# Retention and a mixture of experts in one kernel: gating products one tile later, weight splits and first expert loads reordered

## The chip, the cores and the metric

The kernel runs on one core of a Trainium2 chip. The metric is the device time of one execution in microseconds (us); the median of several runs is compared.

## The reference

The input is q, k and v for 8 batches, 8 heads, 576 positions and a head size of 64. A causal attention with a decay per head (retention, no softmax) gives 4608 rows of 512 numbers. Each row then goes to one of 8 experts.

```python
scores = scale * np.matmul(q, k.transpose(0, 1, 3, 2))
ret = scores * Dmat[None]                # gamma_h ** (i - j) for i >= j, else 0
x = np.matmul(ret, v)                    # -> rows [4608, 512]
...
logits = x @ w_gate
e_idx = np.argmax(logits, axis=1)
gate_w = softmax(logits)[row, e_idx]     # in the reference: exp, sum + 1e-9
eom = 1.0 / (1.0 + np.exp(-(x @ w_output_gate)))
for e in range(E):
    h = np.maximum(x[mask] @ w1[e], 0.0)           # 512 -> 1024
    ye = h @ w2[e]                                 # 1024 -> 512
    out[mask] = gate_w[mask, None] * eom[mask, e, None] * ye
```

## The kernel before, in words

**Attention.** The rows are worked on in 36 tiles of 128 (`NTILE`). The state of a batch is carried in `st_ps` and copied to `stT`; a cycle of 9 tiles (`CPB`) holds two batches. The order on TensorE, ScalarE, VectorE and SyncE is the order of the program (`tc.manual_schedule()`): each engine takes its instructions in that order and waits where a semaphore is missing. Iteration g does, among other things:

- `scores(g + 1)`: 16 products of 64 x 128 into the two PSUM tiles `sc0` and `sc1` (one buffer each), which VectorE masks into `S_sb`;
- `k_rows(g + 1)`: four transpositions into `k_ps`, copied by ScalarE (not for tiles with g % 9 = 8);
- `xnat(g - 1)`: the transposed output `xT` of the tile before is turned back to rows and multiplied with the gate weights in the same products (into `xa` and `xb`, one buffer each); ScalarE copies the rows to `xgrp`, VectorE the logits to `lg`;
- `outT(g)`: the tile's output into `o_ps`, with the state's part and the masked scores' part; VectorE scales it into `xT`;
- `update(g)`: the state (not in tile g % 9 = 8; tile g % 9 = 0 uses no state).

**Gating** is done for groups of four tiles (`GT`). At the end of iteration 4k, `gate1` finds each row's expert on VectorE and builds `oh` (one-hot rows) and the running counts `c1` and `cum`. `gate2`, two small products on TensorE, counts the rows before each row; it stands in `xnat`, that is in iteration 4k+1, and writes into the free end of `xb`. `gate3`, at the end of the same iteration, makes the slots on VectorE and puts four row scatters into the list `todo`; each later iteration issues one on GpSimd (from iteration 30 on, two). The scatters write the rows, with token number and weight, to the DRAM tensor `xs`, one region per expert. With group 5 (`SNAP`) the kernel fixes expert 0's first 360 slots (`CA`): if fewer rows have come by then, filler rows (`fill`, `zx`) take the rest. So expert 0's first part can be computed before all rows are known.

**Weights.** Expert 0's weights are loaded during the attention and each is split in two parts, `hi` on ScalarE (`hi_w`) and `lo` on VectorE (`lo_w`), in the iterations that `wsched` names: (load, `hi`, `lo`).

**Experts.** All products run as three products of split operands. `transp` makes the transposed, split rows; `mm1(e, part, fb)` makes one of 8 blocks of 128 hidden units for part 0 (360 rows for expert 0, 384 loaded) or part 1 (256 rows) and splits it into `hh` (ScalarE) and `hl` (VectorE); `mm2(e, t)` makes the output of one of five row tiles, which ScalarE scales into `y` and GpSimd scatters to the output. Expert 0's first three row tiles are loaded as whole rows (`load_rows`, `x_g`) and transposed on TensorE; every other row tile is loaded in strided quarters by four DMAs (`load_x`, `x_q`) and transposed on VectorE (L221). The DMAs of `read` wait for every scatter issued so far in the program (`scat`). `fill_slots(e)` issues five filler scatters of expert e on GpSimd.

The functions that the change touches:

Of the kernel before, what the change touches and what calls it, by code (L numbers as in the profile page):

```python
# [23 lines left out]
DM = H * D  # L24
# [23 lines left out]
def tile_retention_moe(  # L48
# [101 lines left out]
    XG, XT, HT = {}, {}, {}  # L150
    scat, todo, at = [], [], {}
    pools = {"xt0": xta, "ht0": hpa}

    def read(**kw):
        i = SP.dma_start(**kw)
# [4 lines left out]
    def load_rows(e, t):  # L160
        XG[e, t] = xg.tile([P, DM], F32, name="x_g")
        o, m = e * NT + ROW0[t], ROWS[t]
        read(out=XG[e, t][0:m], in_=xs[o:o + m, 0:DM])

    def load_x(e, t):
# [7 lines left out]
    def load_idx(e, part):  # L173
        ts = range(TA) if part == 0 else range(TA, CT)
        if e == 0 and part == 0:
            for t in ts:
                o, m = ROW0[t], ROWS[t]
                read(out=idx[0:m, e, t], in_=xs[o:o + m, DM:DM + 2].bitcast(I32))
# [28 lines left out]
    def transp(e, t):  # L207
# [7 lines left out]
        if e == 0 and part == 0:  # L215
            src = pools["ps_h"].tile([P, KB, P], F32, name="h_ps")[:, :, 0:m]
# [9 lines left out]
    def mm1(e, part, fb):  # L226
# [8 lines left out]
        for k in range(KB):  # L235
            for a, b in ((wh, xh), (wh, xl), (wl, xh)):
                T.matmul(ps, lhsT=a[:, k, :], rhs=b[:, k, 0:n], start=(j == 0), stop=(j == 3 * KB - 1))  # L237
# [4 lines left out]
    def mm2(e, t):  # L242
# [6 lines left out]
        for fb in range(FB):  # L249
            wh, wl = (a[:, fb % 2, :] for a in W2[e, fb // 2])  # L250
            hh, hl = HT[e, part, fb]
            for a, b in ((hh, wh), (hh, wl), (hl, wh)):
                T.matmul(ps, lhsT=a[:, n], rhs=b, start=(j == 0), stop=(j == 3 * FB - 1))  # L253
# [55 lines left out]
    def scores(g):  # L309
# [4 lines left out]
        for p in range(NP):  # L314
            for r in range(2):
                q, k = (pk[g][64 * r:64 * r + 64, i, P * p:P * p + P] for i in range(2))
                T.matmul(sc[r][:, p], lhsT=k, rhs=q, start=True, stop=True)  # L317
        for r in range(2):
# [41 lines left out]
    def gate1(n):  # L360
# [14 lines left out]
        zo = sm.tile([P, GT, E], F32, name="zo")  # L375
        V.tensor_tensor(out=zo, in0=z, in1=oh, op=ALU.mult)
        zs = sm.tile([P, GT, 1], F32, name="zs")
        V.tensor_reduce(out=zs, in_=zo, op=ALU.add, axis=AX.X)
# [5 lines left out]
        for t in range(GT):  # L384
            V.tensor_tensor(out=c1[:, t + 1] if t < GT - 1 else cum, in0=c1[:, t], in1=oh[:, t], op=ALU.add)
        ex = sm.tile([P, GT, E], F32, name="ex")
# [14 lines left out]
    def gate3():  # L401
        n, oh, c1, ex, zs = gt.pop("pend")
# [3 lines left out]
        V.tensor_tensor(out=sl, in0=r_ps, in1=bs.broadcast_to([P, GT, E]), op=ALU.add)  # L406
        V.tensor_tensor(out=sl, in0=sl, in1=oh, op=ALU.mult)
# [14 lines left out]
        if n == SNAP:  # L422

            V.tensor_copy(cnt[:, 0], c_ps[:, 0:1])
            todo.extend(fill(0, 1, cnt[:, 0:1], float(CA), TA)[0])
            V.tensor_scalar(out=bump, in0=c_ps[:, 0:1], scalar1=-1.0, scalar2=float(CA), op0=ALU.mult, op1=ALU.add)
# [4 lines left out]
    def xnat(g):  # L431
# [7 lines left out]
        if "pend" in gt:  # L439
            gate2(xb[:, 288:512], False)  # L440
# [14 lines left out]
    for n in (512, 512, 256):  # L455
# [3 lines left out]
    wsched = {(1, 0): (5, 8, 9), (1, 1): (10, 14, 15), (1, 2): (15, 18, 19), (1, 3): (20, 24, 25),  # L459
              (2, 0): (29, 32, 33), (2, 1): (30, 33, 34), (2, 2): (31, 34, 35), (2, 3): (34, 36, 36)}  # L460
# [11 lines left out]
    gap = const.tile([1, 1], F32, name="gap")  # L472
    every = {mybir.EngineType.PE, mybir.EngineType.Activation, mybir.EngineType.DVE, mybir.EngineType.SP}
    with tc.manual_schedule():
        S_next = scores(0)
        k_rows(0)
        for g in range(NTILE):
# [6 lines left out]
            if g == 32:  # L484
                for t in range(TA):
                    load_rows(0, t)
                load_idx(0, 0)
# [78 lines left out]
    mm1(0, 0, 0)  # L566
    gate2(ps_t.tile([P, 512], F32, name="t_ps"), True)
    gate3()
# [161 lines left out]
```

## Time and profile before

| | us |
|---|---|
| median of 3 runs | 649.43 (648.3 to 650.15) |
| the profiled execution | 650.73 |
| its span, first to last instruction | 648.9 |
| TensorE matmuls busy | 621.5 (96%) |
| TensorE weight loads busy | 551.9 (85%) |
| VectorE busy | 358.7 (55%) |
| ScalarE busy | 170.8 (26%) |
| GpSimd busy | 166.9 (26%) |
| mean granted TensorE clock | 0.982 of full speed |

The time of an execution is a little longer than the span. The five engines run side by side, so that busy times don't add up. Matmul records overlap (the next starts while the last still drains), and their ends are modelled. In the rows of the profile PE is TensorE, PEld its weight loads, DVE VectorE, ACT ScalarE, POOL GpSimd and SP SyncE, which issues most DMAs; PEq, SPq and so on are the sequencers. A row of the timeline has the start, the duration, the engine, the line, the operation, what it writes and reads, the shapes, and in brackets the idle time before it with what ended it.

### The profile page before, as it was taken

To read this page: it belongs to the slowest core of one execution; us is meant where nothing else is said; L and a number is where in the kernel's file an instruction comes from. 1 tells how busy PE (TensorE), PEld (TensorE's weight loads), DVE (VectorE), ACT (ScalarE), POOL (GpSimd) and SP (SyncE) were. 2 spreads that over 40 slices of the span, in tenths; PEclk is the share of its full clock that TensorE was granted. 3 is DMA by queue.
4 is the path that set the end of the run, shared out by engine and by line. 5 is a ranking of instruction groups with operands and counts; after the bars stand their busy time and mean duration, and the time that the engine had idled before them with its cause. 6 is when DMAs were issued, how large, how long until landed. Compare 5 with 4: busy or idle time off the path is not lost. (4 is left out here: it accounts for less than half of the span.)

```text
span 648.9 us, 12779 instructions
## 1 busy us (share of the span) xinstructions
PE 621.5 (96%) x5127; PEld 551.9 (85%) x5127; DVE 358.7 (55%) x750; ACT 170.8 (26%) x379; POOL 166.9 (26%) x229
## 2 busy tenths in 40 slices
PE   8999999989969699999999999999999999999995
PEld 6888888878859488997997898799799889979974
DVE  3567787677753237773575286267438518625420
ACT  2333433323431122222222222222222222222210
POOL 2244433545426441401501320150110110010011
PEclk9999999989989699999999999999999999999999
DMA  9867686656424545633364183254417416311001
GB/s 323 275 232 251 219 292 231 215 197 240 147 90 129 141 138 162 188 106 127 115 178 130 59 235 88 82 151 117 143 62 212 126 36 186 123 46 65 0 34 43
DMA packets 55610, 96.24 MB, mean 148 GB/s; under 512 B 14736, under 2 KB 36625, under 8 KB 55548
## 3 DMA queue, kind: packets, MB, share of 16 engines
q1 hardware_dynamic: 45836, 72.99, 37.1%
q0 software_dynamic: 9280, 21.36, 9.0%
q10 hardware_dynamic: 432, 1.05, 0.4%
q8 instruction: 41, 0.67, 0.4%
q14 instruction: 21, 0.17, 0.1%
HBM read 74.02 MB, written 30.64 MB: 161 GB/s over the span
## 5 line engine op out<-in xcount | busy, mean ns | idle before, releaser
L237 PE MATMUL h_ps<-xh,w1h 128*128 128x360 f32 (+1 forms) x512 | 157.1, 307 | 2.9 <-ACT xh L223 2.5
L237 PE MATMUL h_ps<-xl,w1h 128*128 128x360 f32 (+1 forms) x512 | 157.0, 307 | 0.3 <-DVE xl L224 0.3
L237 PE MATMUL h_ps<-xh,w1l 128*128 128x360 f32 (+1 forms) x512 | 156.9, 306 | 0.0
L253 PE MATMUL y_ps<-w2h,hh 128*128 128x512 f32 (+1 forms) x320 | 127.2, 397 | 4.8 <-ACT hh L239 4.8
L257 POOL DMA_INDIRECT out_dram<-y,idx x40 | 39.7, 994 | 346.8 <-ACT y L256 333.8
L253 PE MATMUL y_ps<-w2h,hl 128*128 128x512 f32 (+1 forms) x320 | 126.4, 395 | 1.5 <-issue 1.5
L253 PE MATMUL y_ps<-w2l,hh 128*128 128x512 f32 (+1 forms) x320 | 126.4, 395 | 0.0
L240 DVE SCALAR_TENSOR_TENSOR hl<-h_ps,hh 128x360 fp32r<-128x360 f32 (+1 forms) x128 | 58.7, 475 | 101.1 <-ACT hh L239 99.3
L237 PEld LDWEIGHTS h_ps<-xh,w1h 128*128 128x128 f32 x512 | 97.7, 191 | 3.6 <-ACT xh L223 2.7
L239 ACT ACTIVATE hh<-h_ps 128x360 fp32r<-128x360 f32 (+1 forms) x128 | 54.9, 429 | 171.0 <-PE h_ps L237 151.1
L237 PEld LDWEIGHTS h_ps<-xl,w1h 128*128 128x128 f32 x512 | 97.7, 191 | 1.0 <-DVE xl L224 0.7
L237 PEld LDWEIGHTS h_ps<-xh,w1l 128*128 128x128 f32 x512 | 97.5, 190 | 0.0
L253 PEld LDWEIGHTS y_ps<-w2h,hh 128*128 128x128 f32 (+1 forms) x320 | 59.5, 186 | 20.6 <-ACT hh L239 6.2
L224 DVE TENSOR_TENSOR xl<-x_t,xh 128x512 fp32r<-128x512 f32 x37 | 25.6, 692 | 91.1 <-ACT xh L223 90.4
L253 PEld LDWEIGHTS y_ps<-w2h,hl 128*128 128x128 f32 (+1 forms) x320 | 59.5, 186 | 16.5 <-issue 1.3
L253 PEld LDWEIGHTS y_ps<-w2l,hh 128*128 128x128 f32 (+1 forms) x320 | 59.5, 186 | 14.4
L256 ACT ACTIVATE y<-y_ps,idx 128x512 f32<-128x512 f32 (+1 forms) x40 | 27.6, 690 | 146.7 <-issue 77.2
L319 DVE TENSOR_TENSOR S_sb<-sc,cmat_sb 128x512 f32<-128x512 f32 x72 | 46.1, 682 | 17.9 <-PE sc L317 17.9
L185 POOL DMA_INDIRECT xs<-xgrp,sli x36 | 38.3, 1063 | 66.8 <-ACT xgrp L443 20.9
L306 POOL TENSOR_TENSOR vp<-pk,gk_sb 128x512 f32<-128x512 f32 x36 | 37.6, 1044 | 54.0 <-PE st_ps L333 40.5
L185 POOL DMA_INDIRECT xs<-zx,fill x40 | 47.2, 1180 | 9.5 <-issue 9.4
L317 PE MATMUL sc<-pk 64*128 64x128 f32 x576 | 43.7, 289 | 1.8 <-DVE S_sb L319 1.5
(116 smaller groups left out, 669.9 us busy)
## 6 DMA issues: line engine op xcount, KB each, us to landing
st<-in_w_dram SPq DMA_DIRECT2D x64, 512.0 KB
pk<-in_pack_dram SPq DMA_DIRECT2D x32, 768.0 KB
x_q<-xs SPq DMA_DIRECT2D x148, 64.0 KB
gq_sb<-in_gq_dram SPq DMA_DIRECT2D x5, 256.0 KB
pk<-in_pack_dram SPq DMA_DIRECT2D x4, 256.0 KB
pk<-in_pack_dram SPq DMA_DIRECT2D x2, 512.0 KB
xs<-zx,fill POOLq DMA_INDIRECT x40
out_dram<-y,idx POOLq DMA_INDIRECT x40
```

The source lines that it names most:

```text
L185: i = G.indirect_dma_start(out=xs, out_offset=bass.IndirectOffsetOnAxis(ap=at, axis=0), in_=x, in_offset=None, **({} if bound is None else ...
L224: V.tensor_tensor(out=lo, in0=src, in1=hi.bitcast(F32), op=ALU.subtract)
L237: T.matmul(ps, lhsT=a[:, k, :], rhs=b[:, k, 0:n], start=(j == 0), stop=(j == 3 * KB - 1))
L239: A.activation(out=hh, in_=ps, func=AF.Relu)
L240: V.scalar_tensor_tensor(out=hl, in0=ps, scalar=0.0, in1=hh.bitcast(F32), op0=ALU.max, op1=ALU.subtract)
L253: T.matmul(ps, lhsT=a[:, n], rhs=b, start=(j == 0), stop=(j == 3 * FB - 1))
L256: A.activation(out=y, in_=ps, func=AF.Copy, scale=idx.bitcast(F32)[0:m, e, t, 1:2])
L257: G.indirect_dma_start(out=out, out_offset=bass.IndirectOffsetOnAxis(ap=idx[0:m, e, t, 0:1], axis=0), in_=y, in_offset=None, bounds_check= ...
L306: G.tensor_tensor(out=vs[g], in0=pk[g][:, 2].rearrange("p (h d) -> p h d", h=H), in1=gk_sb[:, g % CPB].broadcast_to([P, H, D]), op=ALU.mult)
L317: T.matmul(sc[r][:, p], lhsT=k, rhs=q, start=True, stop=True)
L319: V.tensor_tensor(out=S_sb[:, r], in0=sc[r], in1=m, op=ALU.mult)
```

## The change

- `gate2` leaves `xnat`. It now stands in `scores`, for the tile with g % 4 = 3, behind the score products, so in iteration 4k+2. `gate3` is cut in two: `gate3a` (the slot sum, and for group 5 the copy of the count) follows it directly, ahead of `S_sb`; `gate3b`, the rest, follows `S_sb`. In `gate1` two operations (`zo`, `zs`) move behind the running counts. The scatters of `todo` are issued behind the next tile's preparation, one per iteration, from iteration 26 on two.
- `wsched` has other iterations for most loads and splits of expert 0's weights.
- Expert 0's first rows are loaded one iteration earlier (31) and wait for the scatters issued by iteration 30 only. Their transpositions, with PSUM space from `k_ps`, move into iterations 34 and 35, ahead of the last tile's `xnat`, and `mm1(0, 0, 0)` and `mm1(0, 0, 1)` are placed around that `xnat` and the last gating.
- Expert 0's row tiles 3 and 4 are now loaded as whole rows too and transposed on TensorE, between its second products.
- Expert 1's x tiles are loaded one by one later; the first of the four DMAs of each waits for a matmul on TensorE (`paced`, `pe[0]`: the first product of the block or second product issued last). Their transpositions move behind expert 0's part 1. Expert 1's first weights are split on ScalarE and VectorE (`hi_w`, `lo_w`) in place of VectorE alone (`load_w`).
- Fillers: expert 2's are issued during expert 0's part 1 in place of ahead of it, those of expert e + 2 in place of e + 3 in each later expert.

```diff
-    def read(**kw):
+    def read(paced=False, first=None, **kw):
         i = SP.dma_start(**kw)
-        for j in scat:
+        if paced:
+            tc.add_manual_dep(i.ins, pe[0].name, SYNC, reason="not before TensorE is at this point")
+        for j in scat if first is None else first:
             tc.add_manual_dep(i.ins, j.name, SYNC, reason="reads the rows after every scatter so far")
...
         for a in range(4):
-            read(out=XG[e, t][32 * a:32 * a + 32],
+            read(paced=e == 1 and a == 0, out=XG[e, t][32 * a:32 * a + 32],
...
-        if e == 0 and part == 0:
-            src = pools["ps_h"].tile([P, KB, P], F32, name="h_ps")[:, :, 0:m]
+        if e == 0:
+            src = pools["ps_x"].tile([P, KB, P], F32, name=pools["x_ps"])[:, :, 0:m]
...
                 T.matmul(sc[r][:, p], lhsT=k, rhs=q, start=True, stop=True)
+        if "pend" in gt and g % GT == 3:
+
+            gate2(gt["xb"][:, 288:512], False)
+            gate3a()
         for r in range(2):
             V.tensor_tensor(out=S_sb[:, r], in0=sc[r], in1=m, op=ALU.mult)
...
-    def gate3():
-        n, oh, c1, ex, zs = gt.pop("pend")
+    def gate3a():
+        n = gt["pend"][0]
         r_ps, c_ps = gt.pop("ps")
         bs = base if n <= SNAP else base2
         sl = sm.tile([P, GT, E], F32, name="sl")
         V.tensor_tensor(out=sl, in0=r_ps, in1=bs.broadcast_to([P, GT, E]), op=ALU.add)
+        if n == SNAP:
+            V.tensor_copy(cnt[:, 0], c_ps[:, 0:1])
+        gt["sl"] = sl
+
+    def gate3b():
...
-        if "pend" in gt:
-            gate2(xb[:, 288:512], False)
+        gt["xb"] = xb
...
-    wsched = {(1, 0): (5, 8, 9), (1, 1): (10, 14, 15), (1, 2): (15, 18, 19), (1, 3): (20, 24, 25),
-              (2, 0): (29, 32, 33), (2, 1): (30, 33, 34), (2, 2): (31, 34, 35), (2, 3): (34, 36, 36)}
+    wsched = {(1, 0): (6, 10, 11), (1, 1): (10, 14, 15), (1, 2): (15, 18, 19), (1, 3): (18, 22, 23),
+              (2, 0): (25, 28, 29), (2, 1): (28, 31, 31), (2, 2): (30, 33, 33), (2, 3): (34, 36, 36)}
...
-            if todo:
-                G.memset(gap, 0.0)
-                todo.pop(0)()
             if g + 1 < NTILE:
                 prep(g + 1)
                 S_next = scores(g + 1)
+                if "sl" in gt:
+                    gate3b()
                 k_rows(g + 1)
-            if todo and g >= GT * SNAP + 10:
-                G.memset(gap, 0.0)
-                todo.pop(0)()
+            for _ in range(1 if g < GT * SNAP + 6 else 2):
+                if todo:
+                    G.memset(gap, 0.0)
+                    todo.pop(0)()
+            if g >= NTILE - 2:
+                transp(0, g - NTILE + 2)
             if g > 0:
                 xnat(g - 1)
             outT(g, S_sb, prev)
             update(g)
+            if g == NTILE - 1:
+                transp(0, 2)
             if g % GT == 0 and g > 0:
                 gate1(g // GT - 1)
-            if g % GT == 1 and g > 1:
-                gate3()
             weights(g)
...
+    mm1(0, 0, 0)
     xnat(NTILE - 1)
     gate1(NTILE // GT - 1)
-    for t in range(TA):
-        transp(0, t)
...
-    mm1(0, 0, 0)
+    mm1(0, 0, 1)
     gate2(ps_t.tile([P, 512], F32, name="t_ps"), True)
-    gate3()
+    gate3a()
+    gate3b()
...
-    mm1(0, 0, 1)
...
     for t in range(TA, CT):
-        load_x(0, t)
+        load_rows(0, t)
     load_idx(0, 1)
+    w = [start_w(1, 1, fp) for fp in range(2)]
     fill_slots(1)
-    for t in range(3):
-        load_x(1, t)
+    for fb in range(2, FB):
+        mm1(0, 0, fb)
     load_idx(1, 0)
     load_idx(1, 1)
-    fill_slots(2)
-    for fb in range(2, FB):
-        mm1(0, 0, fb)
-    for t in range(TA):
-        mm2(0, t)
-        if t < CT - TA:
-            transp(0, TA + t)
-        else:
-            transp(1, 0)
+    mm2(0, 0)
+    mm2(0, 1)
+    load_x(1, 0)
+    for t in range(TA, CT):
+        transp(0, t)
+    mm2(0, 2)
+    load_x(1, 1)
...
+            if e == 0:
+
+                if fb in (0, 2):
+                    w.append(start_w(1, 1, 2 + fb // 2))
+                if fb in (1, 3, 5):
+                    load_x(1, 2 + fb // 2)
+                if fb % 2 == 1:
+                    hi_w(*w[fb // 2])
+                    lo_w(*w[fb // 2])
...
-            if fb == 7 and e + 3 < E:
-                fill_slots(e + 3)
-            if e == 0 and fb in (2, 6):
-                transp(1, 1 if fb == 2 else 2)
+            if fb == (7 if e else 4) and e + 2 < E:
+                fill_slots(e + 2)
...
-                if nx:
-                    transp(e + 1, t)
+                for u in (t,) if e else range(3) if t == TA else range(3, CT):
+                    if nx:
+                        transp(e + 1, u)
                 mm2(e, t)
```

More of the change, by code (lines that the diff above doesn't have):

```diff
@@ L177, in load_idx @@
                 o, m = ROW0[t], ROWS[t]
-                read(out=idx[0:m, e, t], in_=xs[o:o + m, DM:DM + 2].bitcast(I32))
+                read(first=first, out=idx[0:m, e, t], in_=xs[o:o + m, DM:DM + 2].bitcast(I32))
         else:
@@ L236, in mm1 @@
             for a, b in ((wh, xh), (wh, xl), (wl, xh)):
-                T.matmul(ps, lhsT=a[:, k, :], rhs=b[:, k, 0:n], start=(j == 0), stop=(j == 3 * KB - 1))
+                i = T.matmul(ps, lhsT=a[:, k, :], rhs=b[:, k, 0:n], start=(j == 0), stop=(j == 3 * KB - 1))
+                if j == 0:
+                    pe[0] = i.ins
                 j += 1
@@ L252, in mm2 @@
             for a, b in ((hh, wh), (hh, wl), (hl, wh)):
-                T.matmul(ps, lhsT=a[:, n], rhs=b, start=(j == 0), stop=(j == 3 * FB - 1))
+                i = T.matmul(ps, lhsT=a[:, n], rhs=b, start=(j == 0), stop=(j == 3 * FB - 1))
+                if j == 0:
+                    pe[0] = i.ins
                 j += 1
```

41 lines of the change are left out of this document (23 added, 18 removed).

## The prediction

> **What bounds the kernel now.** I read the table of stretches first. It gives TensorE's (PE's) busy time and its granted clock per 10 us, and so shows where a saving could lie at all.
>
> ```profile
> 130.00:140.00 10.00, 7.93 (x102) 6.62 (x98) 8.36 (x28) 1.61 (x4) 5.49 (x7) 0.90 0.63 213
> 140.00:150.00 10.00, 10.00 (x140) 9.13 (x140) 5.45 (x14) 3.50 (x9) 3.22 (x6) 0.93 0.54 180
> ...
> 190.00:200.00 10.00, 9.80 (x45) 9.53 (x46) 4.38 (x19) 2.44 (x5) 2.22 (x3) 0.69 0.08 27
> ...
> 210.00:220.00 10.00, 4.31 (x17) 2.65 (x15) 0.53 (x1) 0.47 (x1) 6.30 (x12) 0.83 0.51 113
> 220.00:230.00 10.00, 9.39 (x28) 7.42 (x29) 3.25 (x4) 1.68 (x4) 0.98 (x1) 0.66 0.70 191
> ```
>
> The columns are the stretch, busy time of PE, its weight loads, VectorE (DVE), ScalarE (ACT) and GpSimd (POOL), then the clock. Before 130 and after 230 PE is full at clock 1.00, apart from short waits, so PE's own work sets the time. What can be won lies around 130 to 150, and between 180 and 230, where PE sits idle and then runs at a reduced clock: (1 - 0.90) + (1 - 0.93) over 10 us each is 1.7 us lost to the clock, 190 to 200 loses 3.1, and 210 to 230 loses 1.7 + 3.4.
>
> Second, the waits, summed by engine (us in total, times, longest):
>
> ```profile
> ACT hh L239 <- remote: 14.1, 2, 8.1
> ...
> PE xb L395 <- DVE c L385: 4.1, 8, 0.8
> ...
> DVE xT L355 <- remote: 2.6, 1, 2.6
> ...
> PE xb L437 <- DVE bump L426: 0.6, 1, 0.6
> ```
>
> `xb L395` is the gating product in `xnat`: eight times PE stands still for the running count that DVE is still making. The "remote" ones are releases that came late although the matmul records had ended.
>
> Third, the start of each tile's scores on PE, from the timeline. Scores of tile g+1 stand in iteration g, so two rows bracket one iteration.
>
> ```profile
> 44.65 1.16 PE L317 MATMUL sc<-pk 64*128 64x128 f32 x16
> 48.94 1.16 PE L317 MATMUL sc<-pk 64*128 64x128 f32 x16
> ...
> 87.16 1.16 PE L317 MATMUL sc<-pk 64*128 64x128 f32 x16
> 92.09 1.16 PE L317 MATMUL sc<-pk 64*128 64x128 f32 x16
> 96.24 1.16 PE L317 MATMUL sc<-pk 64*128 64x128 f32 x16
> ...
> 130.89 1.16 PE L317 MATMUL sc<-pk 64*128 64x128 f32 x16
> 137.44 2.67 PE L317 MATMUL sc<-pk 64*128 64x128 f32 x16 [1.35 <-DVE S_sb L319]
> 143.78 1.16 PE L317 MATMUL sc<-pk 64*128 64x128 f32 x16
> ...
> 153.96 1.16 PE L317 MATMUL sc<-pk 64*128 64x128 f32 x16
> 158.71 1.16 PE L317 MATMUL sc<-pk 64*128 64x128 f32 x16
> ...
> 173.54 1.16 PE L317 MATMUL sc<-pk 64*128 64x128 f32 x16
> ```
>
> A full iteration takes 158.71 - 153.96 = 4.75 us; one without a state update (g = 8) 4.29, and the one after it (g = 18, no state product) 4.15.
>
> **The change part by part.** The profiled execution took 650.73 us for a span of 648.9; the median of three runs is 649.43, that is 1.30 below it. I sum savings on the profiled rows and take them off the median.
>
> *A, attention up to the last scores (173.54).* The gating products move from iteration 4k+1 to behind the scores of iteration 4k+2, a tile later, when the count is long made: the 4.1 us of waits go. The products themselves stay. What is late next is DVE: the gate chain still stands before S_sb of tile 4k+2, and the next scores may not overwrite `sc` until S_sb has read it.
>
> ```profile
> 52.21 1.28 DVE L319 TENSOR_TENSOR S_sb<-sc,cmat_sb 128x512 f32<-128x512 f32 x2
> ...
> 90.42 1.28 DVE L319 TENSOR_TENSOR S_sb<-sc,cmat_sb 128x512 f32<-128x512 f32 x2
> ...
> 130.54 0.69 DVE L355 TENSOR_TENSOR xT<-o_ps,gq_sb 128x512 f32<-128x512 f32 x1 [0.33 <-PE o_ps L351]
> 131.15 0.18 DVE L406 TENSOR_TENSOR sl<-xb,csm_sb 128x32 f32<-128x32 f32 x1
> ...
> 133.89 1.69 DVE L429 TENSOR_TENSOR base<-base,bump 128x1 f32<-128x1 f32 x1
> ```
>
> S_sb ends 53.49 - 48.94 = 4.55 us after its scores began, in the other case 91.70 - 87.16 = 4.54. A full iteration of 4.75 has room for that (0.2 us). Group 1 falls into one of 4.15 and loses 0.4, group 3 into one of 4.29 and loses 0.25, group 5 into a short one too, some 0.2. Together -0.85; if the room of 0.2 is missed by as much everywhere, -1.7.
>
> Group 5 (`SNAP`) today costs two iterations of 6.55 and 6.34 us where 4.29 and 4.15 are due: 4.45 lost, 1.7 of it clock. DVE's chain from the slot sum at 131.15 to the end of the row at 133.89, 4.43 us, and then a weight split of 1.28 us, stand before S_sb. Afterwards the sum and the count's copy alone stand ahead of S_sb and the split is moved away, but the rest of the chain still stands ahead of `xT` of tile 26: it starts 1.5 us after the scores do (their 1.16 and the products), runs for 4.43 + 1.28, and two logit copies (about 0.35) and `xT`'s 0.69 follow: 8.3 us. `xnat(26)` wants `xT` one iteration, its scores and a group of transpositions later, 4.29 + 1.16 + 0.45 = 5.9. That is a wait of 2.4 us, or 0.9 if the 1.69 us addition takes the 0.2 of the chain's other rows. I take 2.0, nearer to the long row since POOL's scatters still run beside it, and again 1.7 for the clock: 3.7 against 4.45, +0.75 (between +0.35 and +3.55).
>
> [...] PE waited 0.6 us and then 1.35 us (137.44), and the clock fell (0.90, 0.93). [...]
>
> The splits move: expert 0's first part of w2 is now split at the end of iteration 29, which is 4k+1, when DVE has already run late through group 6's chain. The 1.28 us stand before the slot sum, PE may not write the next `xb` until that has read it: I take -1.0 (0 to -1.4). The other moved splits and their loads fall into tiles that DVE fills with S_sb, `xT` and the copies only, 2.3 of 4.75 us: nothing; without that cover 1.28 each. SP's order of loads moves with them, each three tiles or more ahead of its split but for one (30 to 33).
>
> A: 4.1 - 0.85 + 0.75 - 1.0 = +3.0.
>
> *B, from there to the end of expert 0's first products (208.75).*
>
> ```profile
> 184.08 0.73 PE L437 MATMUL xa<-iw,xT 128*128 128x144 f32 x4 [2.43 <-DVE xT L355]
> ...
> 189.25 0.67 PE L237 MATMUL h_ps<-xh,w1h 128*128 128x360 f32 x1 [2.53 <-ACT xh L223]
> ...
> 208.75 0.39 PE L253 MATMUL y_ps<-w2h,hh 128*128 128x512 f32 x1
> ...
> 212.69 0.40 PE L253 MATMUL y_ps<-w2h,hl 128*128 128x512 f32 x1
> ...
> 220.61 0.79 PE L253 MATMUL y_ps<-w2h,hh 128*128 128x512 f32 x1 [3.70 <-ACT hh L239]
> ...
> 235.33 0.28 PE L237 MATMUL h_ps<-xh,w1h 128*128 128x256 f32 x1
> ...
> 201.06 0.47 ACT L239 ACTIVATE hh<-h_ps 128x360 fp32r<-128x360 f32 x1 [1.50 <-PE h_ps L237]
> 203.03 0.47 ACT L239 ACTIVATE hh<-h_ps 128x360 fp32r<-128x360 f32 x1 [1.50 <-PE h_ps L237]
> ...
> 188.29 0.16 DVE L385 TENSOR_TENSOR cum<-c,oh 128x8 bf16<-128x8 bf16 x1
> ...
> 253.69 1.08 DVE L221 STREAM_TRANSPOSE x_t<-x_q 128x512 f32<-128x512 f32 x1
> ...
> 256.13 1.08 DVE L221 STREAM_TRANSPOSE x_t<-x_q 128x512 f32<-128x512 f32 x1
> ```
>
> The transpositions move from behind the last `xnat` into tiles 34 and 35 (same 12 products), and two blocks of `mm1`, 203.03 - 201.06 = 1.97 us each, are put where PE now waits 2.43 and 2.53 us. Both waits go (+5.0). New ones: the first block waits for the last transposition's two parts on ACT and DVE, below the 256.13 - 253.69 - 1.08 = 1.36 us that they take for a full tile: -1.2; from the start of `xnat(35)` to the end of the count 188.45 - 184.08 = 4.4 us pass, and PE has its own products (1.2) and one block (1.97) meanwhile: -1.2; group 7's chain, another split (33) and three row splits crowd DVE in the last two tiles, -1.2 net of what waits there today. The clock loss of 3.1 shrinks to one window, 1.7: +1.4. B: 5.0 - 1.2 - 1.2 - 1.2 + 1.4 = +2.8; bounds 0 (the late release of 2.6 stays: POOL still runs scatters back to back here) and +5.
>
> *C, expert 0's first three second products (208.75 to 235.33).* Three take 72 matmuls; (212.69 - 208.75) / 17 = 0.232 us each, so 16.7 us, where 26.6 pass. PE idles because ACT's `hh` of blocks 6 and 7 were released 8.1 and 6.0 us late, and then runs at reduced clock. At that time two queues are full:
>
> ```profile
> 212.76 7.47 SPq L155 DMA_DIRECT2D x_q<-xs  x12
> ...
> 197.17 1.26 POOL L185 DMA_INDIRECT xs<-xgrp,sli  x1 [14.39 <-issue]
> ...
> 216.76 0.99 POOL L185 DMA_INDIRECT xs<-zx,fill  x1 [0.25 <-issue]
> ...
> L218 PE MATMUL h_ps<-cmat_sb,x_g 128*128 128x128 f32 (+1 forms) x12 | 1.6, 281 | 0.0
> ```
>
> POOL runs 16 row scatters without a pause, SP issues 20 loads of strided quarters of rows (`x_q`, 12 of them in this row). The change takes both down: expert 0's rest comes as two loads of whole rows, expert 1's x wait for PE's progress, fill 2 moves behind. POOL's run falls to 11. The eight transpositions that then go to PE cost 8 x 1.6 / 12 = 1.06 us. If the late releases are gone: 26.6 - 16.7 - 1.1 = 8.8. I take +8.0, leaving a remainder, since 11 scatters still overlap the rows' loads; bounds 0 and 8.8.
>
> *D, expert 1's transpositions and loads.* Now all five transpositions stand on DVE behind expert 0's last block and the last split. One takes 2.44 us with its two parts (256.13 - 253.69). Starting 2.4 us after the last block, five end at 14.6; PE needs three of them after two second products (24 x 0.232 each, 11.1), which holds, and the last two after one more block of 1.97, at 13.1: a wait of 1.5, less what of the last part is not yet needed: -1.3 (0 to -2). Expert 1's loads get a new wait on SP, for the second and third second product on PE. Behind it on SP stand the other x loads and the last two weight parts of expert 1; these are issued with the first blocks of part 1, and the first of what they bring is used some five blocks later: nothing. Fills of later experts move one expert back, and are still read an expert after they are issued: nothing.
>
> Everything later stays full on PE, so it moves as a whole. Sum: 3.0 + 2.8 + 8.0 - 1.3 = 12.5 us; 649.43 - 12.5 = 636.9.
>
> **The rivals.** (1) *The hold moves along.* Fill 2 has no wait but POOL's order, so it runs right behind the third output scatter, beside expert 1's x loads; if five fills and twelve loads hold releases as 12 and 20 did, C is lost again. For it: the two queues are the same. Against: `h_ps` has four buffers, 5.8 us of cover. 649.4 - (3.0 + 2.8 - 1.3) = 644.9.
>
> (2) *No clock is lost.* If the waits that are left, all under 2.5 us, don't trip the clock, A and B gain 1.7 each: 633.5. For it: at 184.08 PE had waited 2.43 us and the stretch from 190 alone, after the 2.53 us wait, is slow. Against: 137.44. [...]
>
> (3) *Slower: the clock falls in every gate tile.* The place is the new wait of the scores for S_sb. Waits of 0.5 us did not lower the clock, 0.6 and 1.35 close together did; if DVE's chain with the scatters beside it runs 1 us longer, each of eight groups loses 0.5 and a window of 1.7: -17.6 in place of -0.85, so 12.5 - 16.75 = -4.25, 653.7. It decides from about 1.3 us of wait per gate tile. Against: DVE's chain has the same operations as today.
>
> **How the numbers follow.** Forecast 0.53, (1) 0.16, (2) 0.21, (3) 0.07, the remaining 0.03 about unchanged. The range takes in (2) with DVE's short addition (+1.5) and the full C and B (+3): 629; above, (1): 645. About 0.3% (2 us) is what a measurement can tell here. Faster 0.89, same 0.03, slower 0.08.
>
> **What would show it.** Right: no wait of `L395` products in tiles; iterations 4k+1 of 4.75; two short iterations of 4.5; the 72 products of part C with no break; `hh` blocks 6 and 7 released at once; a wait of about 1 us ahead of expert 1's first block of part 1. Wrong: half-clock stretches in tiles 5 to 25, "remote" waits of several us after expert 0's third product, or PE waiting on `x_q`.

## The result, and the profile after

| | us | against the kernel before, same chip |
|---|---|---|
| before, median of 4 | 649.03 (648.3 to 650.15) | |
| after, median of 4 | 639.12 (638.89 to 639.73) | 0.9847 (0.983 to 0.9864) |
| after, the profiled execution | 639.73, span 637.9 | |

The change saves 9.9 us by the medians where 12.5 were forecast; the two profiled executions, which the parts below are read from, differ by 11.0. The four parts of the prediction can be read off TensorE's (PE's) rows in the timeline after: the last scores, expert 0's first block and first second product, the transpositions that now stand between the second products, expert 0's part 1, its last two second products, and expert 1's first blocks.

```profile
169.75 1.16 PE L324 MATMUL sc<-pk 64*128 64x128 f32 x16
...
181.95 0.43 PE L240 MATMUL h_ps<-xh,w1h 128*128 128x360 f32 x1 [2.09 <-ACT xh L226]
...
199.75 0.40 PE L258 MATMUL y_ps<-w2h,hh 128*128 128x512 f32 x1
...
210.87 1.12 PE L221 MATMUL t_ps<-cmat_sb,x_g 128*128 128x128 f32 x8
...
217.35 0.28 PE L240 MATMUL h_ps<-xh,w1h 128*128 128x256 f32 x1
...
229.64 0.40 PE L258 MATMUL y_ps<-w2h,hh 128*128 128x512 f32 x1
...
240.55 0.32 PE L240 MATMUL h_ps<-xh,w1h 128*128 128x360 f32 x1
...
244.47 0.38 PE L240 MATMUL h_ps<-xh,w1h 128*128 128x256 f32 x1 [1.84 <-ACT xh L226]
245.19 0.39 PE L240 MATMUL h_ps<-xl,w1h 128*128 128x256 f32 x1 [0.34 <-DVE xl L227]
```

With the rows of before (173.54, 208.75, 235.33) this gives:

| part | before | after | gain | forecast |
|---|---|---|---|---|
| A, up to the last scores | 173.54 | 169.75 | 3.8 | 3.0 |
| B, to the first second product | 35.2 | 30.0 | 5.2 | 2.8 |
| C, three second products | 26.6 | 17.6 | 9.0 | 8.0 |
| all behind, to the span's end | 413.6 | 420.6 | -7.0 | -1.3 |

So the first three parts gave 18.0 us, more than the 13.8 forecast, and 7.0 of it were lost again behind them. The table of stretches after (columns as before) shows both: the clock is whole where it was reduced, and a new gap with a slow stretch stands at 240.

```profile
130.00:140.00 10.00, 9.67 (x132) 8.44 (x131) 6.63 (x28) 2.52 (x7) 5.44 (x9) 1.00 0.95 316
...
180.00:190.00 10.00, 7.86 (x48) 7.17 (x49) 4.76 (x21) 3.29 (x9) 0.34 (x2) 1.00 0.10 38
...
210.00:220.00 10.00, 10.00 (x60) 8.37 (x59) 1.72 (x3) 2.72 (x5) 2.64 (x5) 1.00 0.58 160
220.00:230.00 10.00, 9.64 (x78) 9.29 (x77) 4.35 (x9) 4.59 (x11) 5.12 (x9) 1.00 0.58 158
240.00:250.00 10.00, 7.82 (x40) 7.21 (x39) 6.24 (x9) 2.77 (x6) 4.98 (x8) 0.83 0.34 127
```

The 2.09 us at 181.95 are a release that comes late, as at the same place before. ScalarE (ACT) and VectorE (DVE) both stand there while GpSimd (POOL) issues the last of four row scatters (the number in brackets is the whole idle time of the engine; `xh` wants the transposition of 179.13, whose last product ends at 179.86, so it comes 1.5 us late):

```profile
179.29 0.96 POOL L188 DMA_INDIRECT xs<-xgrp,sli  x1 [0.22 <-issue]
...
181.33 0.69 DVE L366 TENSOR_TENSOR xT<-o_ps,gq_sb 128x512 f32<-128x512 f32 x1 [3.14 <-PE k_ps L221]
...
181.39 0.51 ACT L226 CAST xh<-k_ps 128x416 fp32r<-128x416 f32 x1 [3.40 <-remote]
```

### The profile page after: what moved, and what is told of

It reads as the page before. It is cut to its first block, busy times and chain, and to the rows that moved or that the text cites. A ratio compares the mean times of both kernels' runs of the same rounds, so it can differ in the third digit from the quotient of the medians.

```text
span 637.9 us, 12795 instructions
## 1 busy us (share of the span) xinstructions
PE 620.4 (97%) x5135; PEld 550.1 (86%) x5135; DVE 353.1 (55%) x748; ACT 173.3 (27%) x387; POOL 166.0 (26%) x229
## 5 line engine op out<-in xcount | busy, mean ns | idle before, releaser
L258 PE MATMUL y_ps<-w2h,hh 128*128 128x512 f32 (+1 forms) x320 | 125.8, 393 | 0.0
L227 DVE TENSOR_TENSOR xl<-x_t,xh 128x512 fp32r<-128x512 f32 x35 | 24.2, 693 | 80.3 <-ACT xh L226 78.2
L324 PE MATMUL sc<-pk 64*128 64x128 f32 x576 | 45.1, 288 | 0.8 <-DVE S_sb L330 0.4
```

Source lines behind the costliest of these rows:

```text
L227: V.tensor_tensor(out=lo, in0=src, in1=hi.bitcast(F32), op=ALU.subtract)
L258: i = T.matmul(ps, lhsT=a[:, n], rhs=b, start=(j == 0), stop=(j == 3 * FB - 1))
```

## The experiments

Each time is a median, with the ratio to the kernel before on the same chip and its 95% interval. The other sessions spread more (before: 648.0 to 652.6), so kernels of different sessions are compared by ratio; the changed kernel's is 0.9847. "C" is the time from the first second product to the first block of part 1, from the profile of that run.

**Half of the change each: the attention part (e1) and the experts' part (e2).** In e1 the code behind expert 0's first two blocks is that of before; in e2 the code ahead of it is. Of the diff in the section on the change, e2 has everything from the lines on that turn `load_x(0, t)` into `load_rows(0, t)`, with `paced` and the row form of `transp(0, t)`; e1 has the rest. Only the first lines of each edit are shown:

```diff
 e1, on the changed kernel
-        load_rows(0, t)
+        load_x(0, t)
...
+    for t in range(3):
+        load_x(1, t)
...
+    fill_slots(2)
 e2, on the kernel before
-        load_x(0, t)
+        load_rows(0, t)
...
-    for t in range(3):
-        load_x(1, t)
...
-    fill_slots(2)
```

> The change up to expert 0's first blocks alone (gating, splits, first loads, transpositions and first two blocks); everything behind them stays as before, with 16 scatters and 20 strided loads together. By the two traces the changed kernel had won 3.8 us up to the last scores and 5.2 us from there to the first second product. Theory 1 (the late releases belong to their traffic and cost TensorE the same wherever it stands): 649.0 - 9.0 = 640.0, with hh of blocks 6 and 7 released 6 to 8 us late and 9 us lost in the first three second products. Theory 2 (the lateness counts only for what TensorE still has to wait for): the loads stand at POOL's scatters, which now start 7 us ahead of the second products in place of 11.6, so that the late stretch falls behind the release of the blocks; part of the 9 us of stage C then goes without any change of loads: 631 to 637. By my prediction's own terms A and B: 649.0 - 5.8 = 643.2.

> The change behind expert 0's first two blocks alone (row loads and TensorE transpositions for expert 0's tiles 3 and 4, expert 1's loads and transpositions later, fills one expert later); attention as before. By the traces C gives 9.0 us, expert 0's part 1 loses 0.8 and expert 1's first blocks 4.2 (a wait of 1.84 and 0.34 us and one stretch at half clock): 649.0 - 4.0 = 645.0. If the 2.6 us that experts 3 to 5 took longer in the changed kernel's trace belong to the change too (fills moved by an expert): 647 to 648. If C needed the attention's change as well (it came from where the traffic falls and not from how much there is of it): 649 or more, with late hh releases in the trace.

Measured: e1 640.36 (0.984, 0.9796 to 0.9884), e2 647.22 (0.9947, 0.9913 to 0.9981). The halves gain 10.4 and 3.4 us by ratio, together more than the whole change: they don't add up. In e1 the late release moved with its traffic:

```profile
201.80 0.40 PE L258 MATMUL y_ps<-w2h,hh 128*128 128x512 f32 x1
...
217.40 0.59 PE L258 MATMUL y_ps<-w2l,hh 128*128 128x512 f32 x1 [1.51 <-issue]
...
217.64 0.69 ACT L263 ACTIVATE y<-y_ps,idx 128x512 f32<-128x512 f32 x1 [13.95 <-remote]
...
226.88 0.28 PE L240 MATMUL h_ps<-xh,w1h 128*128 128x256 f32 x1
```

All `hh` were out in time, yet C still took 25.1 us: `y` of the first product, whose last matmul ended at 207.5, came 10 us late, and PE itself stood four times (the last is shown) with nothing that the profile names as its reason. By C theory 1 holds and theory 2 falls (the time's wide interval alone would leave room for both), though what came late was `y` and not, as theory 1 had it, `hh`. In e2 C fell to 18.4, with the attention of before: so C's gain comes with the experts' part alone. But e2 shows the same wait of 1.84 us at expert 1's first block of part 1 as the changed kernel, and its gain is a third of C, by ratio near the 4.0 us of its first expectation. Its ten executions spread from 643.3 to 651.6, and the profiled one (650.74) is among the slowest: there 5.8 us are lost behind C and 2.4 ahead of it, so that nothing is left of C's 8.2.

**What holds the releases in C: the scatters (e5) or the strided loads (e6).**

```diff
 e5, on the kernel before
-    fill_slots(2)
     for fb in range(2, FB):
...
-            if fb == 7 and e + 3 < E:
-                fill_slots(e + 3)
+            if fb == (7 if e else 4) and e + 2 < E:
+                fill_slots(e + 2)
 e6, on the kernel before: the first of each tile's four DMAs waits for mm2(0, t),
 and none of the twelve waits for the scatters of fill_slots(2)
-    for t in range(3):
-        load_x(1, t)
...
         mm2(0, t)
+        load_x(1, t)
```

> The kernel before with one thing changed: expert 2's five fillers are issued in expert 0's part 1 (and those of expert e + 2 in place of e + 3 later), so that POOL's run ahead of the second products has 11 scatters in place of 16; the 20 strided loads stay where they are. Theory POOL (the long run of scatters holds the releases): stage C (first second product to first block of part 1, 26.6 us before, 17.6 after with 0.9 of transpositions) falls to 17 to 20: 641 to 644. Theory loads (the strided quarters hold them): C stays at 25 to 27: 649. If the lateness needs both at once: C between 20 and 24, since ten of the scatters still meet the loads: 644 to 647.

> The kernel before with one thing changed: expert 1's first three x tiles (12 of the 20 strided loads) are issued one by one at the first, second and third second product on TensorE; POOL's run of 16 scatters and the other 8 loads stay. Theory loads: C falls to 17 to 20, 641 to 644, perhaps with 1 to 2 us given back where VectorE waits for expert 1's first tile. Theory POOL: C stays at 25 to 27, 649. Both needed: C between 20 and 24: 644 to 647.

Measured: e5 642.35 (0.9869, 0.9817 to 0.9922), e6 649.72 (0.9991, 0.9972 to 1.0011). For each kernel the timeline's first row of C, POOL's last filler, the late `hh` of blocks 6 and 7, and the end of C; e5 first, then e6:

```profile
210.01 0.40 PE L253 MATMUL y_ps<-w2h,hh 128*128 128x512 f32 x1
...
211.53 0.98 POOL L185 DMA_INDIRECT xs<-zx,fill  x1 [0.24 <-issue]
...
214.37 0.83 ACT L239 ACTIVATE hh<-h_ps 128x360 fp32r<-128x360 f32 x2 [6.77 <-remote]
...
227.70 0.28 PE L237 MATMUL h_ps<-xh,w1h 128*128 128x256 f32 x1
```

```profile
208.98 0.39 PE L257 MATMUL y_ps<-w2h,hh 128*128 128x512 f32 x1
...
217.17 0.99 POOL L189 DMA_INDIRECT xs<-zx,fill  x1 [0.24 <-issue]
...
220.52 0.83 ACT L243 ACTIVATE hh<-h_ps 128x360 fp32r<-128x360 f32 x2 [13.75 <-remote]
...
235.05 0.28 PE L241 MATMUL h_ps<-xh,w1h 128*128 128x256 f32 x1
```

Five fillers taken out of the run bring C from 26.6 to 17.7 us, twelve of the 20 loads taken away leave it at 26.1. In e6 none of the twelve is issued before 220.7, after the late `hh`, and the other eight are issued from 206.5 to 210.9. The release comes when POOL's run is over: 1.9 us after the last scatter's end in e5 (212.51), 2.4 in e6 (218.16). With eleven scatters the run ends early enough that block 6, which the second product needs as its 19th matmul, is nearly there in time (PE waits 0.7 us in all).

**Do the scatters need any strided load beside them (e11)?** On the changed kernel:

```diff
     fill_slots(1)
+    fill_slots(2)
...
-            if fb == (7 if e else 4) and e + 2 < E:
-                fill_slots(e + 2)
+            if fb == 7 and e + 3 < E:
+                fill_slots(e + 3)
```

> The changed kernel with expert 2's fillers back behind expert 1's, ahead of the second products (16 scatters in a row from about 192.5 to 213), and those of e + 3 in each later expert. The row loads of expert 0 and the late, paced loads of expert 1 stay, so that no strided load is there while the 16 run. Theory (POOL's run alone holds the releases, until 1 to 3 us after its last scatter): C rises from 17.6 to 23 or more: 644 to 648. Rival (a run holds only while the strided quarters are loaded beside it): C stays at 17.6: 638 to 640.

Measured: 642.05 (0.9883, 0.9859 to 0.9908).

```profile
200.59 0.40 PE L258 MATMUL y_ps<-w2h,hh 128*128 128x512 f32 x1
...
212.84 0.98 POOL L188 DMA_INDIRECT xs<-zx,fill  x1 [0.24 <-issue]
...
216.22 1.26 ACT L263 ACTIVATE y<-y_ps,idx 128x512 f32<-128x512 f32 x2 [14.96 <-remote]
...
223.67 0.28 PE L240 MATMUL h_ps<-xh,w1h 128*128 128x256 f32 x1
```

No: C rises to 23.1 us with two whole-row loads and no quarters beside the run, and `y`, due at 206.3, is released 2.4 us after the last scatter's end (213.82). The time rose by less than expected, 2.3 us by ratio with intervals that overlap a little, since 4.0 of C's 5.5 us were won behind it (expert 1's blocks take 29.9 in place of 31.4). The loads may still add to the hold: e1, with the same attention, 16 scatters and the 20 strided loads, has 25.1. What the scatters do to the releases stays open; that the late ones come with the end of the scatters' run is shown (1.9 us after it in e5, 2.4 in e6 and e11). Two other reasons find no support in the traces. From 204 to 228 in e1 and from 203 to 224 in e11 the DMA queues hold no load of instructions. And from 212 to 216 in e11, ahead of the late `y`, the DMA engines are busy for 0.02 of the time, so that full DMA engines don't hold it either.

**The late release in B: the scatter at 179.3 (e4, e7).**

```diff
 e4, on the changed kernel
-            for _ in range(1 if g < GT * SNAP + 6 else 2):
+            for _ in range(1 if g < GT * SNAP + 6 or g > 32 else 2):
 e7, on the changed kernel
             for _ in range(1 if g < GT * SNAP + 6 else 2):
-                if todo:
+                if todo and g < NTILE - 2:
...
-    for f in todo:
+    for k, f in enumerate(todo):
         f()
+        if k == 0:
+            tc.add_manual_dep(scat[-1], pe[0].name, SYNC, ...)
```

> The changed kernel with one row scatter per iteration in place of two from iteration 33 on; two or three scatters move behind the last gating. Theory (the late release at 179 to 181, xT and xh 3.1 and 3.4 us after their waits began, comes from scatters that stand back to back on POOL there): the wait of 2.09 us ahead of the first block of expert 0 falls below 0.6: 639.1 - 1.5 = 637.6. Rival (the release is late for another reason, code or the end of a stage): the wait stays at 2 us: 639.1. Against both: the fills that move 2.6 us later may delay expert 0's row loads, and TensorE then waits for x_g ahead of its eight transpositions (the cover is about 4 us): 640 to 642.

> The changed kernel with the four row scatters of the last group but one held until TensorE begins expert 0's second block (185 us), where they stood back to back at 175.5 to 180.3; nothing else moves. It tells what the earlier try with one scatter per iteration could not, because POOL ran them at the same times there. Theory (xT of the last tile and xh of the third transposition are released 3.1 and 3.4 us after the wait began because of these scatters): the wait of 2.05 to 2.09 us ahead of expert 0's first block falls below 0.6, and no half-clock stretch follows it: about 1.5 us less than the changed kernel where that stretch was not lost, 4 us where it was: 636 to 638. Rival (released late for another reason): the wait stays at 2 us: 639 to 640. The price: the scatters of the last group and the first fillers may come later than 192.5 and the row loads behind them; the cover there is about 4 us.

Measured: e4 640.14 (0.9846, 0.9799 to 0.9893), e7 634.61 (0.9749, 0.9707 to 0.9791). e4 told nothing: POOL begins group 7's scatters at 175.8 there (175.5 in the changed kernel) and runs all four without a pause, with one put into an iteration as with two. In e7 POOL's own order put the waiting scatter last, so that one was held and three stayed:

```profile
178.21 0.96 POOL L188 DMA_INDIRECT xs<-xgrp,sli  x1 [0.31 <-ACT xgrp L459]
...
180.65 0.43 PE L240 MATMUL h_ps<-xh,w1h 128*128 128x360 f32 x1 [0.62 <-ACT xh L226]
...
184.77 0.96 POOL L188 DMA_INDIRECT xs<-xgrp,sli  x1 [5.61 <-DVE lg L464]
...
198.49 0.40 PE L258 MATMUL y_ps<-w2h,hh 128*128 128x512 f32 x1
```

One scatter moved takes the wait from 2.09 to 0.62 us, with the three others in place. B falls to 28.6 us. The same edit in e10 and e12 leaves 0.59 us each. By ratio e7 gains 6.4 us on the changed kernel, more than B's 1.4: of the 4.0 us between the two profiled executions 2.8 lie behind C, where e7's lost no clock. How much of that is the edit's doing isn't shown.

**Term D: expert 1's transpositions (e3).** On the changed kernel:

```diff
                     lo_w(*w[fb // 2])
+                if fb in (1, 2):
+                    transp(1, fb - 1)
...
-                for u in (t,) if e else range(3) if t == TA else range(3, CT):
+                for u in (t,) if e else range(2, 3) if t == TA else range(3, CT):
```

> The changed kernel with expert 1's first two transpositions behind expert 0's blocks 1 and 2 of part 1 in place of behind all eight; three stay behind. Theory (term D: five transpositions of 2.4 us in a row end 2.2 us after TensorE wants the last, and the wait brings a half-clock stretch of 1.7 us): both go, 639.1 - 3.9 = 635.2, no wait over 0.5 us ahead of expert 1's first block of part 1. Rival 1 (VectorE is full in part 1): two times 2.4 us there keep the four h_ps buffers, TensorE waits 1 to 3 us in part 1: 636 to 639. Rival 2 (x of tiles 0 and 1 not there in time): VectorE and ScalarE stand at x_q and TensorE waits longer than now: 640 or more.

Measured: 637.68 (0.9796, 0.9754 to 0.9839). The wait of 1.84 us and its slow stretch are gone from the trace, 1.09 us came in expert 1's seventh block. By ratio that is 3.3 us less than the changed kernel where the theory had 3.9; the intervals overlap a little. With e7's edit as well (e12):

> The changed kernel with both single gains: the scatter at 179.3 held back, and expert 1's first two transpositions behind blocks 1 and 2 of expert 0's part 1. Theory (term D: the wait of 1.83 and 0.34 us at expert 1's first block of part 1 goes, 0.5 to 1.3 us of waits in experts 0 and 1 come in its place): 634.6 - 1 to 2 = 632.5 to 633.6. Rival (VectorE's work in part 1 is only moved, each wait taken away there comes back in expert 1): 634.6.

Measured: 632.82 (0.9743, 0.9715 to 0.9771), against e7's 0.9749: by ratio 0.4 us, where the theory had 1 to 2 and the rival nothing, and the intervals overlap, so that the times don't tell the two apart. In the profiles expert 1's blocks take 27.6 us, 30.1 in e7.

**Fillers spread over the second products (e8).** On the changed kernel, to see whether the later experts' waits come from five fillers in a row:

```diff
-            if fb == (7 if e else 4) and e + 2 < E:
-                fill_slots(e + 2)
+            if e == 0 and fb == 4:
+                fill_slots(2)
...
                 mm2(e, t)
+                if e > 0 and e + 2 < E and t < 4:
+                    for f in fills[e + 2][t + (t > 0):t + 2]:
+                        G.memset(gap, 0.0)
+                        f()
```

> The changed kernel with the fillers of experts 3 to 7 issued behind the second products of the expert two before (two behind the first, one behind each of the next three) in place of five in a row at the start of an expert, where they meet the strided loads of x. In the traces with the change, experts 2 to 6 have lost 1.9 to 3.2 us to waits of first products for a late h_ps, in those without it 0.7 to 1.0. Theory (the runs of fillers beside the strided loads make the releases late, and VectorE's chain with them): at most 0.5 us is lost there: 637 to 638. Rival (the waits come from the order of the loads and splits themselves): the loss stays at 2 to 3 us: 639 to 640.

Measured: 639.89 (0.9831, 0.9789 to 0.9874): by ratio 1.0 us less than the changed kernel, well inside the intervals, so that no gain is shown. Its profile has one such wait, of 1.4 us, where the changed kernel's has three of 1.7 in all.

**Only the parts that pay (e9, e10).** e9 is e1 with e5's edit; e10 adds e7's:

```diff
 e9, on e1
-    fill_slots(2)
...
-            if fb == 7 and e + 3 < E:
-                fill_slots(e + 3)
+            if fb == (7 if e else 4) and e + 2 < E:
+                fill_slots(e + 2)
 e10, on e9
-                if todo:
+                if todo and g < NTILE - 2:
...
+        if k == 0:
+            tc.add_manual_dep(scat[-1], pe[0].name, SYNC, ...)
```

> Only two parts of the change: the attention part (gating, splits, first loads, transpositions and first two blocks), and expert 2's fillers in expert 0's part 1 (those of e + 2 in place of e + 3 later). Expert 0's and 1's loads and transpositions behind expert 0's first blocks are as before: quarters for all, expert 1's not paced, transpositions on VectorE in between. Theory (of the reordered loads only the five fillers count; the rest of that part costs a wait at expert 1's first blocks): C near 17, no wait over 0.5 us between 217 and 250, experts 1 to 6 lose under 1 us: 632 to 634. Rival (the 20 strided loads start beside the 11 scatters and hold hh and y as the 16 did): C 20 to 25: 636 to 640.

> The same, with the row scatter that stood at 179.3 us held until TensorE begins expert 0's second block. Theory: the gains add: 1.5 to 4 us less than without the hold: 629 to 631. Rival (the later scatter, or the loads that now meet the run of eleven, bring a new late release): 632 or more.

Measured: e9 632.33 (0.974, 0.9713 to 0.9766), e10 631.29 (0.9722, 0.9698 to 0.9746). Both beat the changed kernel, whose interval begins at 0.983. C is 16.7 us in both. That e10 is faster than e9 isn't shown: 1.2 us by ratio, the lower end of the theory's 1.5 to 4 missed, and the intervals overlap. e10's table of stretches has no long gap left:

```profile
180.00:190.00 10.00, 9.62 (x59) 8.93 (x60) 5.96 (x30) 3.55 (x10) 0.96 (x1) 1.00 0.08 30
...
210.00:220.00 10.00, 10.00 (x66) 8.71 (x65) 4.49 (x7) 2.48 (x6) 4.43 (x8) 1.00 0.83 223
...
240.00:250.00 10.00, 10.00 (x73) 10.00 (x72) 8.27 (x13) 2.58 (x6) 6.52 (x11) 1.00 0.62 188
```

e9 is faster than the changed kernel by 0.0107 or 6.9 us, without the row loads, the paced loads, the moved transpositions and the moved splits of expert 1's weights.

## Why the prediction was right, and where it was off

The direction, the parts and the range held, and the sum was 2.6 us too good. That it came so near is in part luck: A to C gave 4.2 us more than forecast, and behind them 5.7 more were lost, most of it in one term, D, that was put at 1.3 and was 4.9.

**A, 3.8 against 3.0.** The scores of tiles 0, 26, 30 and 32 on PE in the timeline, before (tile 32's, at 158.71, was shown) and then after:

```profile
5.54 1.16 PE L317 MATMUL sc<-pk 64*128 64x128 f32 x16
...
125.31 1.16 PE L317 MATMUL sc<-pk 64*128 64x128 f32 x16
...
148.53 1.16 PE L317 MATMUL sc<-pk 64*128 64x128 f32 x16
```

```profile
6.04 1.52 PE L324 MATMUL sc<-pk 64*128 64x128 f32 x16
...
124.25 1.16 PE L324 MATMUL sc<-pk 64*128 64x128 f32 x16
...
135.42 0.73 PE L454 MATMUL xa<-iw,xT 128*128 128x144 f32 x4 [0.33 <-DVE xT L366]
...
143.27 1.58 PE L324 MATMUL sc<-pk 64*128 64x128 f32 x16
...
154.72 1.16 PE L324 MATMUL sc<-pk 64*128 64x128 f32 x16
```

The eight waits are gone. The first 26 tiles gain 119.8 - 118.2 = 1.6, as five waits less the two short iterations had been put, 2.3 - 0.65, but with larger parts: from the scores' starts each of the five iterations 4k+1 became 0.64 shorter, 3.2 in all, and the two places of groups 1 and 3 lost 0.63 and 0.49 in place of 0.4 and 0.25. Two terms were off in opposite directions. Tiles 26 to 30, with the count's chain, gain 23.2 - 19.0 = 4.2: PE waits 0.33 us there, not 2.0 with a slow stretch, since the addition that took 1.69 us before takes 0.16. And tiles 30 to 32 lose 11.45 - 10.18 = 1.3 although a gating wait went from them: the split put at -1.0 costs nearly 2 (1.3, and the 0.49 of that wait), by the chain that was named (split, slot sum, `xb`).

```profile
134.15 0.16 DVE L446 TENSOR_TENSOR base<-base,bump 128x1 f32<-128x1 f32 x1
...
150.50 1.28 DVE L142 TENSOR_TENSOR w2l<-st,w2h 128x512 fp32r<-128x512 f32 x2
151.70 0.18 DVE L417 TENSOR_TENSOR sl<-xb,base 128x32 f32<-128x32 f32 x1
...
151.94 0.76 PE L454 MATMUL xb<-iw,xT 128*128 128x144 f32 x4 [0.55 <-DVE sl L417]
```

**B, 5.2 against 2.8.** The late release stayed, as the lower bound had it, and gave the wait of 2.09. Two terms were too dear. The last group's gating cost nothing, since the products of the second block, placed ahead and around it, covered it. And no clock was lost here (1.00 from 180 to 190), where 1.7 had been kept, the price of one stretch of 3.41 us at half clock, such as the kernel before had from 138.08 to 141.49. That second one was not a property of the kernel. e1 and e3 have the same code up to there and the same wait (2.05, 2.04), and lost 2.6 us to the clock, e8 lost 1.3. The stretches of e1 and then of the changed kernel, cut every 3.41 us on the points where each kernel's clock changes:

```profile
177.62:181.03 3.41, 1.69 (x21) 1.34 (x20) 0.31 (x2) 0.23 (x1) 1.96 (x4) 1.00 0.64 240
181.03:184.45 3.42, 3.09 (x9) 2.76 (x10) 0.90 (x2) 0.27 (x1) 0.00 (x0) 0.50 0.01 5
```

```profile
177.51:180.92 3.41, 2.35 (x37) 1.83 (x36) 0.35 (x2) 0.37 (x1) 2.40 (x6) 1.00 0.54 201
180.92:184.33 3.41, 2.19 (x12) 1.94 (x13) 1.19 (x2) 0.51 (x1) 0.00 (x0) 1.00 0.18 69
```

In these traces the clock changes on a grid. In e1 it does so at 181.03, 187.86, 215.17 and 221.99, which are 2, 8 and 2 steps of 3.41 us apart. Most of e1's wait fell into one stretch, PE was busy for 1.69 us of it, and the next two ran at half clock. In the changed kernel the same wait fell across a border and left 2.35 and 2.19. So rival 2 (no clock lost) came true in A and, by the grid, in B of this one execution, and failed at expert 1. What the prediction should have weighed is a price that depends on where a wait falls: the wait of about 2.05 us here cost 0, 1.3 or 2.6 us in different executions. The place alone doesn't settle it. In e2 the wait at expert 1's first block of part 1 lies whole in one stretch, with PE busy for 1.58 us, and the next stretch has the full clock:

```profile
253.25:256.67 3.42, 1.58 (x11) 1.29 (x9) 1.99 (x4) 1.36 (x3) 0.34 (x1) 1.00 0.31 121
256.67:260.08 3.41, 3.07 (x21) 2.87 (x22) 1.79 (x4) 1.21 (x3) 2.19 (x5) 1.00 0.20 73
```

**C, 9.0 against 8.0.** The size was right, the reason half of it. Of the two queues named, POOL's shorter run is what counts (C is 17.7 us in e5, 26.1 in e6, 23.1 in e11). And the late releases are not gone, as the sum had it; they fall where PE has cover. In the changed kernel `hh` of blocks 6 and 7 came at once (the last at 199.94, 7.5 us into POOL's run), but `y` of the first product, due at 205.5, came at 208.49, 2.0 us after the run's end, and PE went on with the second product. The prediction's "8.1 and 6.0 us late" are ACT's idle times; counted from the end of the blocks' last matmuls (206.9 and 208.9) the two `hh` came 6.7 and 11.2 us late.

**D, -4.9 against -1.3.** This is the term that failed: expert 0's part 1 takes 12.3 us in place of 11.5, expert 1's blocks 31.4 in place of 27.2. The length of the five transpositions was right (2.4 us each). Three things were not counted. They begin 3.4 us after the last block, not 2.4, since the blocks of part 1 are now released late while POOL issues fill 2 (rival 1's mechanism, as far as the two rows below show it: PE has its cover of four buffers, the chain of splits on DVE has not). The last part is wanted at once: 1.84 + 0.34. And after the wait, of whose stretch PE was busy for 1.23 us, a whole stretch ran at half clock, 1.7 us: a price that A and B had been given and D had not. Of the five kernels with this wait of 1.8 us the slow stretch followed in three (the changed one, e4, e8) and not in e2 and e7. That transpositions placed earlier take the wait away is shown (e3, e12). Part 1 takes 11.5 us as before in e11, without fill 2 there, and in e5, e9 and e10, with fill 2 but without the moved splits and transpositions; so its loss needs both.

```profile
225.10 0.98 POOL L188 DMA_INDIRECT xs<-zx,fill  x1 [0.24 <-issue]
...
227.21 0.38 ACT L244 ACTIVATE hh<-h_ps 128x256 fp32r<-128x256 f32 x1 [4.72 <-PE h_ps L240]
```

**Behind that, -2.1.** "Everything later stays full on PE, so it moves as a whole" was not quite so: PE waited 1.7 us in all, up to 1.08 at once, for a late `h_ps` in experts 3 to 5 of this execution, 0.4 in one expert before. Other kernels' profiles have between nothing (e9, e10) and 2.1 us (e2) of it. The time behind expert 1's blocks is 364.5 to 367.1 us in the seven kernels with both the moved fillers and the other reordering of the experts' part, and 363.5 to 364.6 in the seven with one of the two or none. So the loss may need both; but each has one profile, spreading the fillers (e8) didn't settle it, and the cause stays open.

**The rivals and the signs.** Rival 1 (the hold moves along) came true in small: part 1 lost 0.8 us, not C's 8. Rival 3 (the clock falls in every gate tile) did not come: the clock is 1.00 up to 245. Of the signs, the products without a wait, the iterations 4k+1 at their due length, the unbroken C, the two `hh` at once and the wait at expert 1 were there; the last was twice the forecast. The two short iterations of 4.5 were not there as such: one took 4.64, for the other an iteration of 4.75 took 5.38.

## What to carry to other kernels

That it was off the path did not make the run of row scatters on GpSimd free (five fewer ahead of the second products took C from 26.6 to 17.7 us in e5): look at what other engines release while it lasts, and cut the run or move it to where nothing waits. When a change has many parts, cost each part alone: here the moved fillers and the attention's order carried all the gain, and the rest of the reordering gave 7 us of it back. Price a wait with the half-clock stretch that followed it in some of these executions (1.7 us behind the 1.84 at expert 1; 0, 1.3 or 2.6 behind the 2.05 in B), and everywhere alike.

## What the runs showed of the hardware

- While GpSimd issued row scatters back to back, releases between engines came up to 13 us late (`hh` of block 6 in e6: due at 207.2, there at 220.52). Around C the late release came 1.9 us (e5), 2.0 (the changed kernel), 2.4 (e6, e11) and 2.7 (e1) after the end of the run's last scatter; in the kernel before, whose run ended at 217.75, block 6's `hh` came at 213.62, 4.1 us ahead of that end, and block 7's at 220.09, 2.3 behind it. PE itself then stood with no visible reason (in C of e1 for 1.19, 1.04 and 1.51 us among others, of e11 for 0.41 and 1.04). With one scatter moved to 184.77 and the other three in place, the wait ahead of expert 0's first block went from 2.09 us (the changed kernel) to 0.62 (e7).
- In the profiles of the kernel before and of the changed kernel the clock changed in steps of 3.41 us, on grids that lie differently: half clock from 138.08 to 141.49, 189.28 to 196.10 and 216.58 to 226.82 before, from 245.77 to 249.19 after. Cut on these grids between 25 and 620 us, the full-clock stretches just ahead of half clock had PE busy for 1.95, 0.88 and 0.89 us before and 1.23 after; one with 1.78 before (182.45 to 185.86) and the one with 2.19 after (180.92 to 184.33) were followed by full clock, as were all with more. Of the two stretches shown above, e1's with 1.69 was followed by half clock and e2's with 1.58 was not.
